# Performer attention and two MoE layers on one core: second products of the last layer moved by a tile, gate logits on column tiles, float64 conversion paced differently

## The chip, the cores and the metric

The program runs on one core of a Trainium2 chip. Its engines are TensorE (PE; its weight loads are shown as PEld), VectorE (DVE), ScalarE (ACT), GpSimd (POOL) and SyncE (SP, which issues most DMAs). Each works through its own instructions in order and waits on semaphores for the others. The metric is the time of one execution in device microseconds; less is better.

## The reference

```python
def phi(x):                       # q and k, scaled by 1/sqrt(sqrt(64)); omega is 128 x 64
    h = einsum('bhsd,md->bhsm', x, omega) - sum(x * x, -1, keepdims=True) / 2
    return exp(h - max(h, -1)) / sqrt(128)
kv  = einsum('bhsm,bhsd->bhmd', phi(k), v);  z = sum(phi(k), axis=2)
x   = (phi(q) @ kv) / (phi(q) @ z + 1e-6)    # 4 x 8 heads x 576 x 64 -> 2304 x 512
P   = exp(x @ w_gate - max)                  # 2304 x 8, then eight times:
#     P /= row sums;  P /= column sums;  P *= 2304 / 8
x   = sum over e of P[:, e:e+1] * (relu(x @ w1[e]) @ w2[e])   # 512 -> 1024 -> 512, 8 experts
h   = x @ w_in                               # 512 -> 2048, weights given as float64
out = (h - tanh(h)) @ w_out                  # 2048 -> 512, float64 weights, output float32
```

## The kernel before

**Attention** comes first, for about 211 us, and leaves x in DRAM as `xd[0]`. It is not changed but for a few instructions at its start.

**The first layer (experts)** takes three blocks of 768 tokens. Every large product is done in a split form: an operand is taken as a high part (cast on ScalarE, `split`, L81) and a low part (difference on VectorE or GpSimd, L82), and three products of these replace one. A block runs over 32 "quads" (8 experts x 4); a quad is seven first products (`product`, tiles a, b, e, L719) with sums and differences between them (tiles t, L742 to L773), which give four tiles h, and then six second products (`l2`, tile l, L836), one per 128 tokens. These six are queued in `ready` and taken out by `second(n)` between the first products of the next quad. Each adds its result into `acc` on VectorE (L856), weighted by the gate's column. At a quarter of a block (quad 8) the next block's x may be loaded (`xgo`); quads 9 and 10 then split it, largely on VectorE (L207, L82, L223).

**The second layer** takes the same three blocks of tokens. It runs over groups of four "shrinks" (`shrink`, tile p, 12 matmuls, L793). After each, u = p squared (ScalarE, L818) and u*p (VectorE, L819) start a polynomial for small values and tanh for the rest: four activations on ScalarE (L803 to L806), four VectorE instructions (L809 to L812). The last step, the split of the result into high h (ScalarE, L815) and low h (GpSimd, L816), is held back until the next shrink has issued its own instructions (`held`). The tiles t of a shrink have two buffers. After a group of four, three second products (l2, 12 matmuls each, for 128 tokens) are appended to `ready`; their results are added into `acc` on VectorE (L850). There are 4 x 2 groups per block, 24 in all, 96 shrinks. What order they get is set here, in the loop over f = 0 to 3:

```python
second(len(ready) - (3, 3, 2, 1)[f])
```

**Background work** is written as generators which `tick()` advances by a step: `wprep` loads and splits weights, `xprep` loads and splits x, and `bg` holds one of two more. First comes `gate`, during quads 0 to 5 of the first block: it loads x again in 12 pieces of 128 x 2 x 384 (`gx`, two buffers, issued on ScalarE's queue), makes logits transposed (8 x 384, L609), copies them, transposes them (L614), and normalizes the table `pt` eight times (tile cs, L649). Then comes `convert`, which turns the float64 weights into float32 by bit operations: 64 jobs, each with a load of `r` (L671), five steps of two VectorE instructions (L683 to L698), and a store. A step is taken at

```python
if bg and not pace[2] and (pace[1] == 1 or pace[0] * 3 % 8 < 3):
```

and `pace[2]` (L926) forbids it in some quads. The transposes of the first layer's finished result (`x2`, L868) wait in `turned`; `turn()` takes out one.

Of the kernel before, what the change touches and what calls it, by code (L numbers as in the profile page):

```python
# [9 lines left out]
F32 = mybir.dt.float32  # L10
# [3 lines left out]
ALU = mybir.AluOpType  # L14
AX = mybir.AxisListType
# [4 lines left out]
def performer_moe_kernel(ctx, tc, q, k, v, omega, wg, w1, w2, win64, wout64, out):  # L20
# [43 lines left out]
    ident = con.tile([P, P], F32, name="ident")  # L64
    ones = con.tile([P, P], F32, name="ones")
    bsq = con.tile([P, 3], F32, name="bsq")
    wgr = con.tile([P, NC, E], F32, name="wgr")
    pt = con.tile([P, NTT, E], F32, name="pt")


# [185 lines left out]
    with ExitStack() as actx, tc.manual_schedule():  # L256
# [44 lines left out]
        nc.scalar.dma_start(om2[:, 1, :], omega)  # L301
        load(0, 1)
        make_identity(nc, ident)
        nc.gpsimd.memset(qn[1][64:, 1:], 0.0)
        nc.gpsimd.memset(kn[1][64:, 1:], 0.0)
        load(1, 0, 1)
# [6 lines left out]
            nc.vector.memset(t[:, :, 1], 1.0)  # L313
        load(0, 2)
        load(1, 2)
        nc.sync.dma_start(wgr, wg.rearrange("(c p) e -> p c e", p=P))

        tps = bank("omT")
        nc.tensor.transpose(tps[:, :M], om2.rearrange("m a d -> m (a d)"), ident)
# [265 lines left out]
    def gate(gtp):  # L585
# [4 lines left out]

        def load(k):
            if k < 2 * NB:
                gx[k] = gtp.tile([P, 2, TB], F32, tag="gx", name=f"gx{k}", bufs=2)
                nc.scalar.dma_start(gx[k], src[:, k % 2, :, (k // 2) * TB : (k // 2 + 1) * TB])

        load(0)
        load(1)
        for _ in range(4):
            yield
        pl = lbank("lgT")  # L600
# [1 line left out]
        for k in range(2 * NB + 1):  # L602
            if k < 2 * NB:
                if k % 2 == 0:
                    ps = lbank(f"lg{k}")
                x = gx.pop(k)
                for c in range(2):
                    i = 2 * (k % 2) + c
                    nc.tensor.matmul(ps[:E, :TB], wgr[:, i], x[:, c], start=(i == 0), stop=(i == 3))  # L609
                load(k + 2)  # L610
            if lg is not None and k % 2 == 0:
                for i in range(TB // P):
                    t = (k // 2 - 1) * (TB // P) + i
                    nc.tensor.transpose(pl[:, E * t : E * (t + 1)], lg[:, i * P : (i + 1) * P], ident[:E, :E])  # L614
            if k % 2 and k < 2 * NB:
                lg = gtp.tile([E, TB], F32, tag="lg", name=f"lg{k}")
                nc.scalar.copy(lg, ps[:E, :TB])
            if k % 2:
                yield
        nc.vector.tensor_copy(pt, pl[:, : NTT * E].rearrange("p (t e) -> p t e", t=NTT))  # L620
# [260 lines left out]
    def tick():  # L881
        next(wprep, None)
        pace[0] += 1
        if pace[3] or pace[0] % 3 == 0:
            next(xprep, None)
        if bg and not pace[2] and (pace[1] == 1 or pace[0] * 3 % 8 < 3):
            try:
                next(bg[0])
            except StopIteration:
                bg.pop(0)  # L890
# [10 lines left out]
    def turn():  # L901
        if turned:
            turned.pop(0)()
# [11 lines left out]
    for st in stages:  # L915
        kind, s = st
        if kind == 0:
            for Q in range(NQ):
                e = Q // NQE
                if s == 0 and Q == NQE + 1:  # L920
# [2 lines left out]
                    phase.close()  # L923
                    pace[1] = 3
                    bg.append(convert(phase.enter_context(tc.tile_pool(name="cvp", bufs=1))))
                pace[2] = pace[1] > 1 and (Q == 0 or Q >= NQ - 2 or s == 0 and Q < NQE + 3)  # L926
                pace[3] = Q < 2 or Q == NQ - 1
                for i in range(7):
                    need(state["n1"] + i, u1, "w")
# [20 lines left out]
        else:  # L950
            for g in range(NGM):
                for j in range(2):
                    hh = []
                    for f in range(GF):
                        for i in range(2):
                            need(state["n1"] + 2 * f + i, u1, "w")
                            need(state["x0"] + 2 * j + i, ux, "x")
                        hh.append(shrink(state["n1"] + 2 * f, j, f"{s}_{g}_{j}_{f}"))
                        if j:
                            spent1.update(state["n1"] + 2 * f + i for i in range(2))  # L960
                        tick()
                        turn()
                        tick()
                        turn()
                        second(len(ready) - (3, 3, 2, 1)[f])
                    for t in range(3):
                        tt = 3 * j + t
                        ready.append(
# [45 lines left out]
```

## Time and profile before

| | us |
|---|---|
| median of three runs | 2248.67 |
| lowest, highest | 2242.39, 2251.53 |
| the profiled execution | 2249.2 |
| its span in the trace | 2247.4 |
| PE busy in the span | 2162.3 (96%) |
| DVE busy | 1792.7 (80%) |
| POOL busy | 1383.4 (62%) |
| ACT busy | 1057.9 (47%) |

Busy is the time in which an engine works at an instruction. TensorE's clock has two levels, 1.2 and 2.4 GHz; the view of windows gives the granted clock as a share of the higher one, and a matmul at the lower level is as busy as at the higher. In a timeline, equal instructions one behind another are merged (x6), and the brackets give the engine's idle time before an instruction and what ended it.

### The profile page before, as it was taken

To read this page: it belongs to the slowest core of one execution; us is meant where nothing else is said; L and a number is where in the kernel's file an instruction comes from. 1 tells how busy PE (TensorE), PEld (TensorE's weight loads), DVE (VectorE), ACT (ScalarE), POOL (GpSimd) and SP (SyncE) were. 2 spreads that over 40 slices of the span, in tenths; PEclk is the share of its full clock that TensorE was granted. 3 is DMA by queue.
4 is the path that set the end of the run, shared out by engine and by line. 5 is a ranking of instruction groups with operands and counts; after the bars stand their busy time and mean duration, and the time that the engine had idled before them with its cause. 6 is when DMAs were issued, how large, how long until landed. Compare 5 with 4: busy or idle time off the path is not lost.

```text
span 2247.4 us, 33143 instructions
## 1 busy us (share of the span) xinstructions
PE 2162.3 (96%) x10782; PEld 1903.3 (85%) x10782; DVE 1792.7 (80%) x3457; ACT 1057.9 (47%) x2577; POOL 1383.4 (62%) x1631
## 2 busy tenths in 40 slices
PE   8998999999999999999999999999999999999998
PEld 6786688899999899799999899899999887878887
DVE  8886487989998798899989798985555677777776
ACT  6775333333333433333333433333333577777775
POOL 5554476676767676676676767676666455454542
PEclk9999999999999999999999999999999999999999
DMA  4442313332323232323232323322122131221210
GB/s 113 126 124 88 111 59 101 104 95 87 103 78 97 92 99 88 104 94 103 79 103 80 101 85 104 106 87 74 59 76 66 61 111 45 99 71 54 88 43 29
DMA packets 184381, 195.70 MB, mean 87 GB/s; under 512 B 53392, under 2 KB 142992, under 8 KB 184208
## 3 DMA queue, kind: packets, MB, share of 16 engines
q1 hardware_dynamic: 177200, 184.09, 26.0%
q10 hardware_dynamic: 7008, 9.51, 1.3%
q8 instruction: 85, 1.39, 0.3%
q14 instruction: 88, 0.72, 0.1%
HBM read 171.00 MB, written 22.54 MB: 86 GB/s over the span
## 4 chain that ended last, share of the span: by engine, by line
PE 65%; DVE 9%; ACT 8%; issue 4%; POOL 3%; DMA 2%; SPq 0%; ACTq 0%; DVEq 0%; POOLq 0%
PE l L836 33%; PE b L719 12%; PE a L719 8%; PE e L719 8%; PE p L793 2%; POOL h L816 2%; DVE t L819 2%; ACT t L804 1%; ACT th L803 1%; ACT t L806 1%; ACT t L805 1%; POOL u L82 1%; ACT h L815 1%; DMA gx<-xd 1%; DVE acc L856 1%
## 5 line engine op out<-in xcount | busy, mean ns | idle before, releaser
L836 PE MATMUL l<-v,h 128*128 128x512 f32 x4320 | 1072.7, 395 | 35.1 <-ACT h L815 18.6
L836 PEld LDWEIGHTS l<-v,h 128*128 128x128 f32 x4320 | 807.5, 189 | 209.2 <-ACT h L815 25.3
L82 POOL TENSOR_TENSOR v<-rs,v 128x512 fp32r<-128x512 f32 x216 | 287.6, 1335 | 334.7 <-PE l L836 174.8
L856 DVE SCALAR_TENSOR_TENSOR acc<-l,pt,acc 128x512 f32<-128x512 f32 x540 | 397.6, 744 | 120.3 <-PE l L836 118.6
L82 POOL TENSOR_TENSOR u<-s,u 128x256 fp32r<-128x256 f32 x384 | 297.0, 784 | 132.7 <-ACT u L81 107.8
L719 PE MATMUL b<-x,u 128*128 128x384 f32 x1728 | 354.2, 340 | 11.1 <-DVE t L746 6.6
L719 PEld LDWEIGHTS b<-x,u 128*128 128x128 f32 x1728 | 309.9, 189 | 29.7 <-DVE t L746 9.7
L81 ACT CAST u<-s 128x256 fp32r<-128x256 f32 x384 | 154.2, 405 | 264.6 <-POOL s L161 236.4
L816 POOL TENSOR_TENSOR h<-t,h 128x384 fp32r<-128x384 f32 x96 | 112.5, 1172 | 238.4 <-ACT h L815 235.1
L82 POOL TENSOR_TENSOR u<-rq,u 128x256 fp32r<-128x256 f32 x288 | 228.5, 793 | 26.2 <-ACT u L81 24.9
L719 PE MATMUL a<-x,u 128*128 128x384 f32 x1152 | 234.4, 338 | 0.6 <-ACT xo L517 0.6
L719 PE MATMUL e<-x,u 128*128 128x384 f32 x1152 | 232.8, 336 | 0.0
L793 PE MATMUL p<-x,u 128*128 128x384 f32 x1152 | 226.0, 350 | 0.0
L793 PEld LDWEIGHTS p<-x,u 128*128 128x128 f32 x1152 | 216.2, 199 | 5.4
L719 PEld LDWEIGHTS a<-x,u 128*128 128x128 f32 x1152 | 206.3, 188 | 9.0 <-ACT xo L517 1.0
L719 PEld LDWEIGHTS e<-x,u 128*128 128x128 f32 x1152 | 203.6, 189 | 1.3 <-issue 1.3
L730 ACT ACTIVATE h<-b 128x384 fp32r<-128x384 f32 x96 | 47.2, 491 | 257.8 <-DVE b L768 254.5
L81 ACT CAST v<-rs 128x512 fp32r<-128x512 f32 x240 | 147.5, 621 | 37.6 <-PE l L836 36.9
L730 ACT ACTIVATE h<-t 128x384 fp32r<-128x384 f32 x96 | 50.4, 525 | 243.8 <-DVE t L755 243.8
L81 ACT CAST u<-rq 128x256 fp32r<-128x256 f32 x288 | 117.4, 408 | 1.6 <-ACT xo L870 1.6
L803 ACT ACTIVATE th<-p 128x384 f32<-128x384 f32 x96 | 47.2, 491 | 114.5 <-DVE t L819 114.5
L809 DVE TENSOR_TENSOR th<-p,th 128x384 f32<-128x384 f32 x96 | 53.6, 558 | 53.5 <-ACT th L803 53.5
(138 smaller groups left out, 3088.1 us busy)
## 6 DMA issues: line engine op xcount, KB each, us to landing
rq<-in_moe_w_dram SPq DMA_DIRECT2D x96, 512.0 KB, 4.0
rs<-in_moe_w_dram SPq DMA_DIRECT2D x192, 256.0 KB, 2.8
rqi<-win SPq DMA_DIRECT2D x24, 512.0 KB, 5.1
rs<-wout SPq DMA_DIRECT2D x48, 256.0 KB, 2.8
xt<-xd SPq DMA_DIRECT2D x24, 384.0 KB, 5.9
r<-in_moe_w_in_dram SPq DMA_DIRECT2D x32, 256.0 KB, 3.3
r<-in_moe_w_out_dram SPq DMA_DIRECT2D x32, 256.0 KB, 3.3
xd<-xo SPq DMA_DIRECT2D x32, 144.0 KB, 1.8
```

The source lines that it names most:

```text
L81: nc.scalar.copy(dst[:, 0], src)
L82: eng.tensor_tensor(dst[:, 1], src, dst[:, 0].bitcast(F32), ALU.subtract)
L719: nc.tensor.matmul(ps[:, :TB], u[:, wi, c], x[:, xi, c], start=(start and m == 0), stop=(stop and m == 5), skip_group_check=True,)
L730: nc.scalar.activation(h[:, 0], src, AF.Relu)
L793: nc.tensor.matmul(ps, u1[f + i][:, wi, c], ux[state["x0"] + 2 * t + i][:, xi, c], start=(m == 0), stop=(m == 11))
L803: nc.scalar.activation(th, ps, AF.Tanh)
L804: nc.scalar.activation(gb, u, AF.Square, bias=bsq[:, 1:2])
L809: nc.vector.tensor_tensor(th, ps, th, ALU.subtract)
L816: nc.gpsimd.tensor_tensor(lo, s, hi.bitcast(F32), ALU.subtract)
L819: nc.vector.tensor_tensor(s, u, ps, ALU.mult)
L836: nc.tensor.matmul(ps, hh[f][:, hi, t : t + P], u2[n + f][:, wi], start=(i == 0), stop=(i == len(todo) - 1))
L856: V.scalar_tensor_tensor(a, ps, p[:, e : e + 1], a, ALU.mult, ALU.add)
```

## The change

It has three parts. In the second layer `second` leaves one more product in the queue at the third and the fourth shrink, and the second `turn()` of each shrink is gone. In the gate, the four products of a piece of 384 tokens no longer add up in 8 rows of one bank: each goes to 32 columns of its own of TensorE's array and 32 rows of its own of the result (weights padded with zeros to 32 columns), and instead of a transpose a product with `sel` (128 x 8, each column with a one at its place in each of the four groups) sums the four and transposes at once. The pieces of x take the five buffers of `xtp` instead of two of their own, four ahead. The conversion takes 11 steps in 32 ticks instead of 12, may start one quad earlier, and rests in quads 9 and 10 of each block.

```diff
-    wgr = con.tile([P, NC, E], F32, name="wgr")
+    wgr = con.tile([P, NC, P // NC], F32, name="wgr")
+    sel = con.tile([P, E], F32, name="sel")
...
+        nc.vector.tensor_reduce(sel, ident.rearrange("p (g e) -> p e g", g=NC)[:, :E], AX.X, ALU.add)
...
+        nc.vector.memset(wgr, 0.0)
+        nc.sync.dma_start(wgr[:, :, :E], wg.rearrange("(c p) e -> p c e", p=P))
...
-                gx[k] = gtp.tile([P, 2, TB], F32, tag="gx", name=f"gx{k}", bufs=2)
+                gx[k] = xtp.tile([P, 2, TB], F32, tag="x", name=f"gx{k}")
...
-        load(0)
-        load(1)
+        for k in range(4):
+            load(k)
...
-                    nc.tensor.matmul(ps[:E, :TB], wgr[:, i], x[:, c], start=(i == 0), stop=(i == 3))
-                load(k + 2)
+                    g = P // NC * i
+                    nc.tensor.matmul(
+                        ps[g : g + P // NC, :TB], wgr[:, i], x[:, c], start=True, stop=True, tile_position=(0, g)
+                    )
+                load(k + 4)
...
-                    nc.tensor.transpose(pl[:, E * t : E * (t + 1)], lg[:, i * P : (i + 1) * P], ident[:E, :E])
+                    nc.tensor.matmul(
+                        pl[:, E * t : E * (t + 1)], lg[:, i * P : (i + 1) * P], sel, start=True, stop=True
+                    )
...
-                lg = gtp.tile([E, TB], F32, tag="lg", name=f"lg{k}")
-                nc.scalar.copy(lg, ps[:E, :TB])
+                lg = gtp.tile([P, TB], F32, tag="lg", name=f"lg{k}")
+                nc.scalar.copy(lg, ps[:, :TB])
...
-        if bg and not pace[2] and (pace[1] == 1 or pace[0] * 3 % 8 < 3):
+        if bg and not pace[2] and (pace[1] == 1 or pace[0] * 11 % 32 < 11):
...
-                pace[2] = pace[1] > 1 and (Q == 0 or Q >= NQ - 2 or s == 0 and Q < NQE + 3)
+                pace[2] = pace[1] > 1 and (Q == 0 or Q >= NQ - 2 or s == 0 and Q < NQE + 2 or NQ // 4 < Q < NQ // 4 + 3)
...
                         tick()
                         turn()
                         tick()
-                        turn()
-                        second(len(ready) - (3, 3, 2, 1)[f])
+                        second(len(ready) - (3, 3, 3, 2)[f])
```

How the instructions move, at three places. In these rows lines and buffer numbers are those of the two programs, so that L819 of before is L827 of after.

The SP queue where the conversion's first two loads (r) stand; rq and rs are loads of the experts' first and second weights. Before, row by row:

```order
L104 DMA rq<-in_moe_w_dram 128x4x256
L109 DMA rs<-in_moe_w_dram 128x512 x2
L104 DMA rq<-in_moe_w_dram 128x4x256
L109 DMA rs<-in_moe_w_dram 128x512 x2
L104 DMA rq<-in_moe_w_dram 128x4x256
L671 DMA r_0_4463<-in_moe_w_in_dram 128x512
L671 DMA r_1_4465<-in_moe_w_in_dram 128x512
L109 DMA rs<-in_moe_w_dram 128x512
```

After:

```order
L105 DMA rq<-in_moe_w_dram 128x4x256
L110 DMA rs<-in_moe_w_dram 128x512 x2
L105 DMA rq<-in_moe_w_dram 128x4x256
L110 DMA rs<-in_moe_w_dram 128x512
L679 DMA r_0_4300<-in_moe_w_in_dram 128x512
L679 DMA r_1_4302<-in_moe_w_in_dram 128x512
L110 DMA rs<-in_moe_w_dram 128x512
L105 DMA rq<-in_moe_w_dram 128x4x256
L110 DMA rs<-in_moe_w_dram 128x512
```

Before, the two loads of r come after 11 loads of rq and 20 of rs from the program's start; after, they come behind 9 of rq and 17 of rs.

VectorE in the second layer, from the end of the fourth shrink of a group (predicated copy into t) to the second shrink of the next; acc is the addition of a second product, t<-t,p is u*p. Before:

```order
L812 COPY_PREDICATED t_0_2_1_3_20796<-t_0_2_1_3_20793,th_2_1_3_20792 128x384
L850 TENSOR_TENSOR acc_0_1_20043<-l_20815,acc_0_1_20043 128x512
L819 TENSOR_TENSOR t_0_3_0_0_20850<-t_0_3_0_0_20847,p_3_0_0_20832 128x384
L809 TENSOR_TENSOR th_3_0_0_20846<-p_3_0_0_20832,th_3_0_0_20846 128x384
L810 SCALAR_TENSOR_TENSOR t_0_3_0_0_20850<-t_0_3_0_0_20849,t_0_3_0_0_20850 128x384
L811 SCALAR_TENSOR_TENSOR t_0_3_0_0_20850<-t_0_3_0_0_20848,t_0_3_0_0_20850 128x384
L812 COPY_PREDICATED t_0_3_0_0_20850<-t_0_3_0_0_20847,th_3_0_0_20846 128x384
L850 TENSOR_TENSOR acc_0_2_20109<-l_20869,acc_0_2_20109 128x512
L819 TENSOR_TENSOR t_0_3_0_1_20904<-t_0_3_0_1_20901,p_3_0_1_20886 128x384
```

After:

```order
L820 COPY_PREDICATED t_0_2_1_3_20782<-t_0_2_1_3_20779,th_2_1_3_20778 128x384
L858 TENSOR_TENSOR acc_0_0_20021<-l_20801,acc_0_0_20021 128x512
L827 TENSOR_TENSOR t_0_3_0_0_20836<-t_0_3_0_0_20833,p_3_0_0_20818 128x384
L817 TENSOR_TENSOR th_3_0_0_20832<-p_3_0_0_20818,th_3_0_0_20832 128x384
L818 SCALAR_TENSOR_TENSOR t_0_3_0_0_20836<-t_0_3_0_0_20835,t_0_3_0_0_20836 128x384
L819 SCALAR_TENSOR_TENSOR t_0_3_0_0_20836<-t_0_3_0_0_20834,t_0_3_0_0_20836 128x384
L820 COPY_PREDICATED t_0_3_0_0_20836<-t_0_3_0_0_20833,th_3_0_0_20832 128x384
L858 TENSOR_TENSOR acc_0_1_20094<-l_20855,acc_0_1_20094 128x512
L858 TENSOR_TENSOR acc_0_2_20115<-l_20872,acc_0_2_20115 128x512
L827 TENSOR_TENSOR t_0_3_0_1_20907<-t_0_3_0_1_20904,p_3_0_1_20889 128x384
```

An addition follows the fourth shrink in both; after the first shrink there are two in place of one.

VectorE in the second layer, behind the third shrink of a group where it also splits a weight tile v. Before:

```order
L812 COPY_PREDICATED t_0_2_1_2_20738<-t_0_2_1_2_20735,th_2_1_2_20734 128x384
L82 TENSOR_TENSOR v_20753<-rs,v_20753 128x512
L850 TENSOR_TENSOR acc_0_0_19988<-l_20761,acc_0_0_19988 128x512
L819 TENSOR_TENSOR t_0_2_1_3_20796<-t_0_2_1_3_20793,p_2_1_3_20778 128x384
L809 TENSOR_TENSOR th_2_1_3_20792<-p_2_1_3_20778,th_2_1_3_20792 128x384
```

After:

```order
L820 COPY_PREDICATED t_0_2_1_2_20741<-t_0_2_1_2_20738,th_2_1_2_20737 128x384
L83 TENSOR_TENSOR v_20756<-rs,v_20756 128x512
L827 TENSOR_TENSOR t_0_2_1_3_20782<-t_0_2_1_3_20779,p_2_1_3_20764 128x384
L817 TENSOR_TENSOR th_2_1_3_20778<-p_2_1_3_20764,th_2_1_3_20778 128x384
L818 SCALAR_TENSOR_TENSOR t_0_2_1_3_20782<-t_0_2_1_3_20781,t_0_2_1_3_20782 128x384
```

The addition between the split of v and the next u*p is gone from this place. On TensorE the four shrinks p and the three second products l of a group stood in the order p l p p l p l; they now stand in the order p l l p p p l. In the gate the order of TensorE's instructions stays as it was. The transposes x2 at the start of the second layer come one behind each of eight shrinks, where they came two behind each of four. In the whole program the last step of the conversion moves from quad 78 to quad 89, counted over the three blocks.

## Rows read from the trace of the kernel before

**Rows 1.** view of windows: us of stretch, busy per engine (x instructions), clock, DMA, GB/s.

```profile
211.74:261.40 49.66, 44.20 (x192) 26.47 (x192) 15.04 (x32) 14.24 (x36) 19.95 (x26) 1.00 0.48 144
347.28:369.01 21.73, 18.39 (x80) 16.36 (x78) 12.21 (x25) 5.95 (x15) 10.61 (x14) 0.84 0.22 73
384.65:421.42 36.77, 32.14 (x158) 28.02 (x157) 33.20 (x52) 11.01 (x28) 23.58 (x26) 1.00 0.37 122
499.84:687.47 187.63, 187.63 (x937) 169.31 (x936) 171.62 (x297) 68.27 (x168) 130.50 (x156) 1.00 0.30 93
895.18:934.50 39.32, 34.44 (x157) 30.07 (x156) 33.70 (x52) 10.96 (x28) 23.88 (x26) 0.91 0.35 110
1408.34:1442.10 33.76, 32.32 (x158) 27.88 (x157) 29.86 (x49) 11.01 (x28) 22.34 (x26) 1.00 0.40 133
1505.00:1677.00 172.00, 172.00 (x860) 155.17 (x859) 99.87 (x166) 64.21 (x155) 113.88 (x143) 1.00 0.21 68
1843.00:2217.00 374.00, 349.36 (x1653) 308.30 (x1654) 287.43 (x480) 276.86 (x594) 181.30 (x174) 0.96 0.20 65
```

**Rows 2.** waits of PE: who waited for whom, us in total, times, longest.

```profile
PE l L836 <- ACT h L815: 18.6, 12, 2.7
```

**Rows 3.** timeline of the last layer: start, us, engine, line, op, [idle before].

```profile
1785.80 0.55 DVE L819 TENSOR_TENSOR t<-t,p 128x384 f32<-128x384 f32 x1 [2.45 <-ACT t L818]
...
1878.25 0.56 DVE L819 TENSOR_TENSOR t<-t,p 128x384 f32<-128x384 f32 x1 [0.30 <-POOL h L816]
...
1889.97 2.92 PE L836 MATMUL l<-v,h 128*128 128x512 f32 x12
...
1891.18 1.25 DVE L82 TENSOR_TENSOR v<-rs,v 128x512 fp32r<-128x512 f32 x1
...
1892.35 0.67 DVE L850 TENSOR_TENSOR acc<-l,acc 128x512 f32<-128x512 f32 x1
...
1901.08 0.68 DVE L850 TENSOR_TENSOR acc<-l,acc 128x512 f32<-128x512 f32 x1
...
1902.05 0.56 DVE L819 TENSOR_TENSOR t<-t,p 128x384 f32<-128x384 f32 x1 [0.29 <-POOL h L816]
...
1915.44 0.56 DVE L819 TENSOR_TENSOR t<-t,p 128x384 f32<-128x384 f32 x1 [0.29 <-POOL h L816]
...
2234.07 0.73 PE L836 MATMUL l<-v,h 128*128 128x512 f32 x2 [1.72 <-ACT h L815]
```

**Rows 4.** timeline of the SP queue, 320 to 352 us.

```profile
323.15 12.96 SPq L109 DMA_DIRECT2D rs<-in_moe_w_dram  x2
...
349.80 0.93 SPq L671 DMA_DIRECT2D r<-in_moe_w_in_dram  x2
```

**Rows 5.** timeline of DVE at the first conversion step.

```profile
354.48 0.82 DVE L683 TENSOR_SCALAR ct<-r 128x256 uint32<-128x256 uint32 x1 [6.04 <-issue]
```

**Rows 6.** page, part 6: DMA issues, xcount, KB each, us to landing.

```profile
r<-in_moe_w_in_dram SPq DMA_DIRECT2D x32, 256.0 KB, 3.3
```

**Rows 7.** timeline of quads 9, 10 of blocks 0 and 1.

```profile
401.30 1.66 PE L836 MATMUL l<-v,h 128*128 128x512 f32 x6 [2.22 <-DVE acc L856]
...
407.51 1.37 DVE L697 TENSOR_SCALAR ct<-ce 128x256 f32<-128x256 uint32 x1
...
410.93 1.31 PE L719 MATMUL b<-x,u 128*128 128x384 f32 x6 [2.06 <-DVE t L746]
...
904.36 0.83 ACT L81 CAST x<-xt 128x768 fp32r<-128x768 f32 x1 [6.55 <-DMA xt<-xd]
...
909.96 2.29 PE L719 MATMUL b<-x,u 128*128 128x384 f32 x6 [3.84 <-DVE t L754]
```

**Rows 8.** groups by line, PE: xcount, busy, mean ns, idle before.

```profile
L609 PE MATMUL lg<-gx,wgr 128*8 128x384 f32 x48 | 17.3, 486 | 5.0 <-DMA gx<-xd 4.9
...
L649 PE MATMUL cs<-cs,ones 128*128 128x8 f32 x16 | 2.7, 241 | 3.5 <-DVE cs L645 3.4
L614 PE MATMUL lgT<-ident,lg 8*128 8x8 f32 x18 | 2.1, 209 | 0.0
```

More of the change, by code (lines that the diff above doesn't have):

```diff
@@ L315, in performer_moe_kernel @@
         load(1, 2)
-        nc.sync.dma_start(wgr, wg.rearrange("(c p) e -> p c e", p=P))
+        nc.vector.memset(wgr, 0.0)
+        nc.sync.dma_start(wgr[:, :, :E], wg.rearrange("(c p) e -> p c e", p=P))
         tps = bank("omT")
```

## The prediction

> **What bounds the kernel now.** I read the view of windows first, cut at the first matmul of a quad's product a [rows 1]. From quad 16 to quad 28 TensorE is busy all of 187.63 us: twelve quads at 15.63 us each, so in clean stretches of the first layer TensorE is the bound, although VectorE is busy 171.62 us of it. Four stretches are longer. Quad 7 takes 21.73 us instead of 15.63. The quads 9 and 10 of the three blocks of tokens (quads 9+10, 41+42, 73+74 in the count over blocks) take 36.77, 39.32 and 33.76 us instead of 31.27. The gate's stretch (quads 0 and 1) takes 49.66 us. The last layer (1843 to 2217) has TensorE busy 349.36 of 374 us, and its mean granted clock is 0.96.
>
> Then the waits of TensorE [rows 2]: the largest is that of second products for h, 18.6 us on ScalarE's part alone. It looks like the prize of the first part of the change. The timeline says otherwise. In the last layer each shrink begins on VectorE with u*p. From 1878.25 to 1915.44 eight shrinks pass, 37.19 us, 4.65 us each [rows 3]. TensorE does not set this pace: in the window it idles 24.6 us and loses about 15 us more to the lower of its two clock levels (0.04 of 374), so its own work at the full level would be some 334 of 374 us, about 33 us per eight shrinks. VectorE's u*p waits for POOL's h (0.30 and 0.29 us idle before it, ended by POOL h), POOL's h waits for ScalarE's cast of h, that cast stands in ScalarE's order behind the four activations of the next shrink, and those wait for VectorE's u*p. That is a ring over three engines which TensorE only feeds. A wait of TensorE for h inside it is the ring's spare time seen from the other side.
>
> **First part: the last block's second products one tile later.** The number of products, casts and additions is the same. On TensorE the product that stood behind the third shrink of four now stands behind the first shrink of the next four, as the second of two. Hence h is wanted one shrink later and the 18.6 us may well vanish from that line, or shift to another; but the ring turns at its own pace, so they are worth almost nothing by themselves. What counts is where the ring's own engines get other work. Per eight shrinks:
> - Twice VectorE now has two additions in a row (second order fence). One takes 0.68 us, and the row of 1901.08 ends at 1901.76 with 0.29 us idle before u*p at 1902.05 [rows 3]. A second one starts about 0.6 us after the first and overfills that gap by about 0.3 us: +0.6 for the two.
> - Once the addition behind a split of v goes (third fence). There VectorE has no spare time: the split of 1.25 us, then the addition, 0.67, with nothing idle between [rows 3]. About -0.6.
> - A fourth cast of u falls into a slot that had three. +0.1.
>
> So +0.1 us per eight shrinks, +1 us over the layer's twelve such groups; bounds -5 (the additions all hide) and +12 (1 us per group, as much as that costliest slot is over the others). The Trainium skill (SBUF — State Buffer, SBUF: two separate sides) states that VectorE and GpSimd take a shared pair of ports as an exclusive lock, held for the whole instruction by whichever starts first. By that rule a fourth split on POOL can hold VectorE up once more in each group, and the sum would be nearer the upper bound; the split of v at 1.25 us beside POOL agrees with it.
>
> At the layer's start the transposes of the first layer's result come one per shrink instead of two. Now u*p of the third shrink comes after 2.45 us idle on ScalarE's square, which stands behind two copies [rows 3]; half as many copies there, but some in shrinks that had none: -2 (bounds -6 and +2). At the end TensorE waits 1.72 us for the last h [rows 3]; one product more stands ahead of it, but that h comes no sooner: -1 (bounds -1.7 and 0). Sum of the part: -2 us.
>
> **Second part: the conversion.** Each step is two VectorE instructions as before, 320 steps. Three things move.
> - It starts in quad 5 instead of 6, and its first loads move on the SP queue past three slab loads and two quad loads (first fence). Now VectorE sits 6.04 us on the first load, which the SP queue only issued at 349.80 because it stood behind slab loads that waited for buffers [rows 4, 5]. After the change the loads stand behind the slab load issued at 323.15, ahead of the one that held the queue until about 336, while VectorE wants them one clean quad before 347.28, near 331. Such a load lands 3.3 us after issue [rows 6], so the wait goes: 21.73 - 15.63 = -6.1 us, lower clock level included (0.84 in that window). Bounds 0 and -6.1.
> - It pauses in quads 9 and 10 of each block, where the next block's x is split. First block: TensorE idles 2.22 us on an addition and 2.06 us on VectorE's t; conversion steps, one of them 1.37 us, stand right ahead [rows 7]. The second goes, of the first 1 us stays: -4.5 of the 5.5 that the pair is too long. Second block: the 3.84 us are mostly the load of x itself, since ScalarE idles 6.55 us on that DMA and VectorE behind it [rows 7]; conversion steps and the lower clock level (0.91 in that window) come on top: -4.3 of 8.05. Third: -2.0 of 2.49. Sum -10.8; bounds -6.8 (only the steps that stand right before a stall) and -16.0 (all the excess).
> - About eleven of 64 jobs move to quads 78 to 88. There VectorE is busy 99.87 of 172 us; with them it comes to the 171.62 of 187.63 under which TensorE did not idle [rows 1]. Nothing; if that cover fails, up to +2.5, a pair of quads like the third.
>
> **Third part: the gate.** Before, 24 products of 8 columns of weights run one behind another: 48 instructions, 17.3 us. 18 transposes take 2.1 us, and waits for gx 4.9 us [rows 8]. Afterwards four products stand on four column tiles of the array. No row shows column tiles. If they do not overlap: 0; if each pair runs as one: -8.65, half of 17.3. I take the middle, -4.3. The 18 selector products contract over 128 rows in full fp32, two instructions each: by the row of cs (16 instructions, 2.7 us) 36 take 6.1 us, +4.0; at the present 2.1 us, 0; I take +2.6, nearer to cs, which has the same shape. Four loads are issued ahead instead of two, and the issue no longer holds ScalarE until the last products are done: -3.5 of the 4.9 (bounds 0 and -4.9); not all, because the 12 loads of 384 KB still have to come beside the weights. Entering and leaving the tiles at 22 borders: 0 to +3.7 (0.17 us each, one whole small instruction by the row of cs); I take +0.8, near 0, since the borders of today's products show nothing of the kind. Sum -4.4; bounds -13.5 and +8. The rest of the chain behind the gate and the stages after it shift with it, since TensorE takes them up in order. The reduction that makes sel and the clearing of wgr stand at the very start, where TensorE waits for its first load anyway: nothing. The Trainium skill (TensorEngine Tiling (Array Packing), Key Properties) states that tiles run independently and that a change of the tiling mode drains the engine. By the first statement the gate comes out near its lower bound, by the second near the upper; no run here shows either yet.
>
> **Sum.** -2.0 - 6.1 - 10.8 - 4.4 = -23.3 us against the profiled execution's 2249.2 us (span 2247.4): 2225.9. The median of the runs shown is 0.5 lower, so 2225 us.
>
> **Rivals.**
> - Last layer bound by TensorE after all (0.08): then the deferral frees the idle time and the lost clock of [rows 1], up to 40 us over the layer: about 2187. For it: the largest wait of the whole trace is exactly this one. Against: where u*p idles in that group POOL's h or ScalarE ends it, never a product.
> - Column tiles give nothing and pay their borders (0.18): gate +4 instead of -4.4: 2233.
> - The conversion's stalls mostly stay (0.12): the first load still comes late (0 instead of -6.1) and the pauses bring only -6.8: 2235. For it: the second block's stall is a DMA's.
> - Slower (0.05): VectorE's two additions in a row. The second waits for the second of two products of about 2.8 us; VectorE has everything else of the ring queued behind it. Today the product begun at 1889.97 is over at 1892.89, 8.2 us ahead of its addition at 1901.08 [rows 3]. A second one of 2.9 us leaves 5.3; it decides if the lead falls by more than that: then up to 2.5 us are added in each of 23 half groups, +57, about 2282. Against: TensorE has some 4 us to spare in every eight shrinks.
>
> **How the numbers follow.** The forecast has 0.57. Its own range is 2212 to 2236 (the terms' bounds rarely fall on one side together). 0.5% is about what a measurement can tell from no change, 11.2 us: faster is below 2237.4. The forecast gives 0.55 of its 0.57 to faster, the gate rival 0.10 of 0.18, the conversion rival 0.05 of 0.12, the first rival all. Faster 0.78, same 0.16, slower 0.06. The range 2208 to 2240 leaves out the first rival, the slower one and the ends.
>
> **What would show it.** Quad 7 at 15.6 us and no long idle of VectorE before the first conversion step; the pairs at about 32, 35 and 31.8 us; the gate's stretch near 45 us with selector products of about 4.7 us; in the last layer a pace of 4.65 us per shrink, give or take 0.1, while TensorE's wait for h moves behind the fourth shrink. A pace below 4.5 us would refute the ring as the bound; a stretch of the gate above 50 us would refute the tiles' gain; a wait of TensorE of 2 us or more in quads 9 and 10 of the first block would refute the pauses' gain.

## The result

The changed kernel takes 2221.4 us (median of four runs, 2219.1 to 2222.7) against 2245.5 (2242.3 to 2251.5) for the kernel before, on the same chip: ratio 0.9888, 95% interval 0.9862 to 0.9915, so 24 us faster, with 19.1 to 31.0 as the interval. The forecast was 2225, in a range of 2208 to 2240. The two profiled executions stand 27.2 us apart (2249.2 and 2222.0; spans 2247.4 and 2220.2); the one of before is 3.7 us above its kernel's median, so about 3 of these 27.2 us belong to the execution and not to the change.

The sum came out near the forecast. But its terms for the gate and the ends of the last layer were off, and the term for the pauses was nearly right in size for another reason than the one given, as the experiments show. First the trace of the changed kernel. The view of windows, cut at the first matmul of a quad's product a, answers [rows 1] row by row (same columns):

```profile
209.74:249.91 40.17, 38.19 (x210) 27.56 (x210) 15.00 (x32) 14.18 (x36) 19.95 (x25) 1.00 0.53 178
336.04:351.68 15.64, 15.64 (x80) 14.11 (x79) 13.98 (x25) 6.13 (x15) 12.06 (x15) 1.00 0.28 94
367.32:398.60 31.28, 31.28 (x158) 28.22 (x157) 23.82 (x38) 12.12 (x30) 22.69 (x26) 1.00 0.36 118
476.80:664.48 187.68, 187.68 (x938) 169.33 (x937) 166.56 (x288) 68.06 (x168) 131.33 (x156) 1.00 0.28 89
872.21:908.25 36.04, 32.94 (x158) 29.54 (x157) 23.00 (x38) 12.17 (x30) 22.55 (x26) 0.95 0.33 106
1381.84:1413.12 31.28, 31.28 (x158) 28.22 (x157) 19.71 (x35) 12.37 (x30) 21.22 (x26) 1.00 0.39 127
1476.00:1648.00 172.00, 172.00 (x860) 155.19 (x859) 150.75 (x262) 63.08 (x154) 119.82 (x144) 1.00 0.27 88
1814.00:2188.00 374.00, 351.71 (x1696) 311.16 (x1696) 287.75 (x481) 278.02 (x596) 184.17 (x174) 0.97 0.20 65
```

- The gate's stretch has shrunk from 49.66 to 40.17 us.
- Quad 7 is a clean quad (TensorE busy in all of it), 15.64 us (was 21.73).
- Quads 9 and 10 take 31.28 us (was 36.77), 41 and 42 take 36.04 (was 39.32), 73 and 74 take 31.28 (was 33.76). In the first and the third block TensorE is busy in all of it. In the second it still idles about 3 us.
- The clean stretch is as it was, 15.64 us per quad. In the late quads, where the moved conversion steps now are, VectorE is busy for 150.75 of 172 us (99.87 before), and TensorE stays busy for all 172.
- In the last layer TensorE is as idle as before: 351.71 of 374 us busy, 349.36 before.

That last row already says that the deferral moved little. The waits of TensorE (who waited for whom, us in total, times, longest), which answer [rows 2]:

```profile
PE l L844 <- ACT h L823: 18.1, 13, 6.9
PE l L844 <- ACT xo L878: 9.2, 2, 4.9
PE l L844 <- POOL h L824: 7.6, 13, 0.7
...
PE l L844 <- DVE acc L856: 3.5, 2, 2.4
```

The wait for ScalarE's h was 18.6 us and is 18.1. Between the layer's ends it fell from 13.6 to 10.2 us (350 us of each trace), and a wait of 3.5 us for an addition (acc) came instead. At the layer's end it has grown from [rows 3]'s 1.72 to 6.9 us, and at its start the second products wait 9.2 us for copies of the transposed x (xo), where it was 1.7. Counted by place, the waits did not go away but moved: before, 26.1 of the 29.4 us that second products of this layer waited came behind the third shrink of four; now all but the 9.2 us come behind the fourth, 29.2 us with the end's 6.9.

The timeline of the last layer, u*p on VectorE, ring and end, answers [rows 3]:

```profile
1764.41 5.49 PE L844 MATMUL l<-v,h 128*128 128x512 f32 x12 [4.26 <-ACT xo L878]
...
1850.18 0.55 DVE L827 TENSOR_TENSOR t<-t,p 128x384 f32<-128x384 f32 x1 [0.30 <-POOL h L824]
...
1887.30 0.55 DVE L827 TENSOR_TENSOR t<-t,p 128x384 f32<-128x384 f32 x1 [0.31 <-POOL h L824]
...
1891.91 0.55 DVE L827 TENSOR_TENSOR t<-t,p 128x384 f32<-128x384 f32 x1
...
1929.01 0.55 DVE L827 TENSOR_TENSOR t<-t,p 128x384 f32<-128x384 f32 x1
...
2206.24 10.33 PE L844 MATMUL l<-v,h 128*128 128x512 f32 x36 [6.94 <-ACT h L823]
```

From 1891.91 to 1929.01 eight shrinks pass: 37.10 us, 4.64 each, against 4.65 before. The place of TensorE's second products has changed, and u*p still waits for GpSimd's h where it did (1850.18, 1887.30). The row at 1764.41 is the start of the layer: a second product waits 4.26 us for the copy of a transpose. The last one is the end: the final 36 matmuls begin after 6.94 us of idling and take 10.33 us; the granted clock of the window 2196 to 2217 is 0.84.

The groups of TensorE by line, 205 to 262 us (count, busy us, mean ns, idle before), answer [rows 8]:

```profile
L613 PE MATMUL lg<-gx,wgr 128*32 128x384 f32 x48 | 9.2, 497 | 1.5 <-DMA gx<-xd 1.5
...
L620 PE MATMUL lgT<-sel,lg 128*128 128x8 f32 x36 | 4.9, 257 | 0.0
```

The gate's products take 9.2 us in place of 17.3, the selector products 4.9 where the transposes took 2.1, the waits for gx 1.5 in place of 5.0.

The SP queue and VectorE at the first conversion step answer [rows 4, 5]:

```profile
300.76 10.05 SPq L110 DMA_DIRECT2D rs<-in_moe_w_dram  x2
...
312.35 0.86 SPq L679 DMA_DIRECT2D r<-in_moe_w_in_dram  x2
...
321.89 0.75 DVE L864 SCALAR_TENSOR_TENSOR acc<-l,pt,acc 128x512 f32<-128x512 f32 x1 [0.47 <-PE a L727]
322.56 0.85 DVE L691 TENSOR_SCALAR ct<-r 128x256 uint32<-128x256 uint32 x1
```

The load is issued at 312.35, and the first step stands 10 us later with no idle time in front of it.

Where the 27.2 us went, read from the starts of quads and of the dense layer in the two traces: gate -9.45, quad 7 -6.09, quads 9 to 11 of the three blocks -5.71, -3.55 and -2.71 (each sum takes in the quad behind the pair, which had been some 0.25 us over a clean one), attention -2.0, dense layer +2.0, the rest +0.3. The attention's 2 us are not shown to come from the change: the first quad starts at 209.7 to 212.4 us in the seven traces with the gate's part, which adds a few instructions at the attention's start, and at 211.6 to 212.8 us in the six without it. Each of these differences is read from one trace on either side. The gate's stretch repeats well with one exception: it is 48.9 to 49.6 us in the five traces with the old gate, and 39.6 to 40.2 in six of the seven with the new one; in the seventh (e4) it is 43.8, at a granted clock of 0.92. Quad 7 varies more, from 19.9 to 21.7 us in the four traces with the conversion's old start and rate.

### The profile page after: what moved, and what is told of

Read it like the earlier page. It is cut to its first block, busy times and chain, and to the rows that moved or that the text cites. A ratio compares the mean times of both kernels' runs of the same rounds, so it can differ in the third digit from the quotient of the medians.

```text
span 2220.2 us, 33171 instructions
## 1 busy us (share of the span) xinstructions
PE 2143.8 (97%) x10800; PEld 1898.6 (86%) x10800; DVE 1789.6 (81%) x3459; ACT 1059.2 (48%) x2577; POOL 1387.6 (63%) x1631
## 4 chain that ended last, share of the span: by engine, by line
PE 66%; ACT 10%; DVE 9%; issue 3%; POOL 2%; DMA 1%; DVEq 0%; SPq 0%; ACTq 0%; POOLq 0%
PE l L844 34%; PE b L727 13%; PE e L727 9%; PE a L727 8%; DVE t L827 2%; ACT t L812 2%; ACT th L811 2%; ACT t L814 2%; POOL h L824 1%; ACT t L813 1%; ACT h L823 1%; DVE t L819 1%; ACT v L82 1%; DVE t L818 1%; DVE acc L858 1%
## 5 line engine op out<-in xcount | busy, mean ns | idle before, releaser
L844 PE MATMUL l<-v,h 128*128 128x512 f32 x4320 | 1067.4, 396 | 39.8 <-ACT h L823 18.1
L801 PE MATMUL p<-x,u 128*128 128x384 f32 x1152 | 216.8, 344 | 0.0
L801 PEld LDWEIGHTS p<-x,u 128*128 128x128 f32 x1152 | 208.9, 194 | 3.4
```

The source lines that it names most:

```text
L801: nc.tensor.matmul(ps, u1[f + i][:, wi, c], ux[state["x0"] + 2 * t + i][:, xi, c], start=(m == 0), stop=(m == 11))
L844: nc.tensor.matmul(ps, hh[f][:, hi, t : t + P], u2[n + f][:, wi], start=(i == 0), stop=(i == len(todo) - 1))
```

## The experiments

All times are medians of four to eleven runs beside the kernel before on the same chip, unless said otherwise. Ratios are to the kernel before, with their 95% interval.

**Each part by itself.** e1 is the changed kernel with the deferral undone:

```
-                        second(len(ready) - (3, 3, 3, 2)[f])
+                        turn()
+                        second(len(ready) - (3, 3, 2, 1)[f])
```

> The changed kernel with its first part undone: the second products of the dense layer stand where they stood before, and the transposes come two per shrink again; gate and conversion stay changed. Theory (a ring over ScalarE, VectorE and GpSimd sets the pace): eight shrinks take 37.1 to 37.2 us as in both kernels, and the time is 2219 to 2221 us against 2221.4, since the second layer, from its first product to the end, took 473.7 us before and 475.7 after. Rival (TensorE's wait for h was the cost): the layer gets longer by 10 us or more, 2232 or above. Rival (the deferral did harm that other parts hid): below 2217.

Measured: 2220.6 us, ratio 0.9889 (0.9873 to 0.9904), beside 0.9888 with the deferral. Eight shrinks take 37.2 us. From its first product to TensorE's last the layer takes 473.3 us here, 472.0 to 474.5 in the other seven traces that have the old order and all products (the kernel before among them), and 475.0 and 473.6 in the changed kernel and in e6 below, which have the deferral. So the deferral is worth nothing that can be measured, neither in the time nor in the layer's own length: the theory held.

e2 is the kernel before with the gate's part alone, e3 with the conversion's part alone (the diff's lines for each, nothing else).

> The kernel before with the gate's part alone. Theory (the gain of the gate stays to the end, since TensorE takes the work in order): quads 0 and 1 take 40.2 us in place of 49.6, and the time falls by 9 to 10, to about 2236 from 2245.5. Rival (the weights' slabs are then late, or the conversion's first load stalls for longer, so part is given back): 2239 to 2243, with quad 7 longer than 21.7 us.

> The kernel before with the conversion's part alone. Theory: quad 7 falls from 21.7 to 15.6 us, the quads 9 to 11, 41 to 43 and 73 to 75 fall by 5.7, 3.6 and 2.7: 18 us in all, 2227.5. Rival (some of that came from the gate's earlier end, which gives the slab loads more lead): quad 7 or the second block's pair stay longer, 2231 to 2236.

Measured: e2 2238.1 us, ratio 0.9968 (0.9955 to 0.9981), -7 us; e3 2228.7 us, 0.9930 (0.9914 to 0.9945), -16 us. Together 23 of the 24 us. In e2 the gate's stretch is 40.0 us, and the conversion's first load is still late (quad 7: 20.8 us, not the longer one of the rival). The quads 9 and 10 become 1.8 us longer than before, but 41 and 42 become 2.1 us shorter, so the trace does not show that any of the gain is given back. The time lies between theory and rival. In e3 quad 7 takes 15.6 us and the three pairs 31.3, 35.2 and 31.3: the conversion's gain does not need the gate's.

**What sets the pace of the dense layer.** e8 leaves out a third of the second products (the product of h's low part), so TensorE has less to do and everything else is as it was. It ran a single time; the pace is read from its trace:

```
-        todo = [(hi, wi, f) for f in range(len(hh)) for hi, wi in ((0, 0), (0, 1), (1, 0))]
+        todo = [(hi, wi, f) for f in range(len(hh)) for hi, wi in ((0, 0), (0, 1), (1, 0))[: 3 - kind]]
```

> The changed kernel without the third of the three products (low part of h by high part of the weights) in the second products of the dense layer: 12 matmuls of 36 are left out for each four shrinks, some 2.8 us of TensorE's work, 5.6 us per eight shrinks. Theory (the ring sets the pace, TensorE has that time to spare): eight shrinks still take 37.1 us, and the time stays within 5 us of 2221, with TensorE idle for longer. Rival (TensorE with its waits sets the pace): 31.5 to 34 us per eight shrinks and 2155 to 2190.

Measured: 2218.9 us. The timeline of u*p, eight shrinks apart, and the window 1820 to 2170 (columns as above):

```profile
1849.88 0.55 DVE L827 TENSOR_TENSOR t<-t,p 128x384 f32<-128x384 f32 x1 [0.28 <-POOL h L824]
...
1886.95 0.55 DVE L827 TENSOR_TENSOR t<-t,p 128x384 f32<-128x384 f32 x1 [0.29 <-POOL h L824]
```

```profile
1820.00:2170.00 350.00, 290.32 (x1345) 256.04 (x1344) 269.60 (x449) 261.24 (x562) 176.96 (x168) 0.91 0.21 69
```

37.07 us per eight shrinks, the same as with all products. In the same window of the changed kernel TensorE is busy 329.21 us; here 290.32. Nearly 39 us of its work are gone and the time is the same: TensorE does not set the pace, as the theory had it.

e4 loosens a link of the ring. In the trace of the changed kernel, tanh starts at the end of u*p each time, and ScalarE's other three activations and the cast of h stand behind tanh. VectorE in turn waits for tanh, since it takes tanh's result first. The waits of ScalarE from 1820 to 2170, those of VectorE from 1843 to 2190, and the timeline of one shrink:

```profile
ACT th L811 <- DVE t L827: 85.8, 74, 2.3
```

```profile
DVE th L817 <- ACT th L811: 41.9, 75, 0.6
```

```profile
1890.86 0.48 ACT L826 ACTIVATE t<-p 128x384 f32<-128x384 f32 x1
...
1891.91 0.55 DVE L827 TENSOR_TENSOR t<-t,p 128x384 f32<-128x384 f32 x1
...
1892.49 0.49 ACT L811 ACTIVATE th<-p 128x384 f32<-128x384 f32 x1 [1.15 <-DVE t L827]
1892.88 0.61 ACT L812 ACTIVATE t<-t,bsq 128x384 f32<-128x384 f32 x1
...
1893.39 0.60 ACT L813 ACTIVATE t<-t,bsq 128x384 f32<-128x384 f32 x1
```

The two squares gb and ga need only ScalarE's own square of p. So they go ahead of tanh, and VectorE takes tanh's result third in place of first (the same edit in both lists):

```
-            nc.scalar.activation(th, ps, AF.Tanh)
             nc.scalar.activation(gb, u, AF.Square, bias=bsq[:, 1:2])
             nc.scalar.activation(ga, u, AF.Square, scale=CS, bias=bsq[:, 0:1])
+            nc.scalar.activation(th, ps, AF.Tanh)
...
-            nc.vector.tensor_tensor(th, ps, th, ALU.subtract)
             nc.vector.scalar_tensor_tensor(s, gb, B1, s, ALU.add, ALU.mult)
             nc.vector.scalar_tensor_tensor(s, ga, A1, s, ALU.add, ALU.mult)
+            nc.vector.tensor_tensor(th, ps, th, ALU.subtract)
```

> The changed kernel with one edit in the shrink: ScalarE does the two squares gb and ga before tanh, and VectorE uses tanh's result third in place of first. In the trace tanh starts each time at the end of VectorE's u*p (88.4 us of waits in 347), and everything else of ScalarE stands behind it; the two squares need only ScalarE's own result. Theory (the ring sets the pace, and this is a link of it): the pace falls from 4.64 us per shrink to what TensorE needs, some 4.2 (33.5 per eight), and the time by 30 to 42 us, to 2180 to 2191. Rival (TensorE with its lower clock and its waits for h is the bound): the pace stays at 4.6, the time within 5 us of 2221. Rival (VectorE is next, since th comes later and the copy behind it too): 4.4 us per shrink, about 2200.

Measured: 2179.0 us, ratio 0.9707 (0.9690 to 0.9723): 66 us below the kernel before and some 41 below the changed one, by the order of two lists. The timeline of u*p in e4, eight shrinks apart, and its window 1790 to 2140:

```profile
1852.19 0.54 DVE L827 TENSOR_TENSOR t<-t,p 128x384 f32<-128x384 f32 x1
...
1886.16 0.54 DVE L827 TENSOR_TENSOR t<-t,p 128x384 f32<-128x384 f32 x1
```

```profile
1790.00:2140.00 350.00, 347.59 (x1744) 312.82 (x1743) 323.97 (x486) 284.70 (x607) 194.01 (x181) 1.00 0.21 70
```

Eight shrinks take 33.97 us, 4.25 each, and TensorE is busy 347.59 of 350 us at a granted clock of 1.00. Now TensorE is the bound. The waits of ScalarE in e4, from 1800 to 2150:

```profile
ACT th L813 <- DVE t L827: 61.8, 77, 1.7
```

Tanh still waits for u*p in nearly every shrink, but the two squares are done by then. VectorE's wait for tanh, 41.9 us before the edit, is gone. The two lists were changed together, and neither was run alone, so how they share the gain is not shown.

Why tanh waits for u*p at all is argued from the kernel's lines, no run took it apart: the two instructions share nothing but p, which both read from the same PSUM bank. The Trainium skill (PSUM — Partial Sum Buffer, PSUM bank collisions raise a hardware error) states that two engines may not touch the same partitions of one bank at the same time, reads included, and that the compiler's scheduler puts a dependency between them. The trace agrees with such a dependency: u*p ends at 1891.91 + 0.55 = 1892.46 and tanh starts at 1892.49, and 74 such waits come to 85.8 us.

With TensorE as the bound the deferral might have become worth something. e5 is e4 with the deferral undone, by the lines of e1:

> The kernel of e4 (tanh behind the two squares) with the deferral undone. In e4 eight shrinks take 33.9 us and TensorE is the bound of the second layer. Theory (the deferral is worth something only where TensorE sets the pace, since then a wait for h is no longer spare time of the ring): 35 us or more per eight shrinks and 2187 to 2205 against 2179. Rival (worth nothing in either order, because h now comes earlier by itself): 2176 to 2183.

Measured: 2177.8 us, ratio 0.9699 (0.9686 to 0.9713); eight shrinks take 33.9 us. The rival was right: the deferral is worth nothing in either order. e4 and e5 can't be told apart, and both beat the kernel before and the changed one.

**What the gate's gain is made of.** e7 is the kernel before with the loads alone changed: gx from the pool of x, four ahead.

```
-                gx[k] = gtp.tile([P, 2, TB], F32, tag="gx", name=f"gx{k}", bufs=2)
+                gx[k] = xtp.tile([P, 2, TB], F32, tag="x", name=f"gx{k}")
...
-        load(0)
-        load(1)
+        for k in range(4):
+            load(k)
...
-                load(k + 2)
+                load(k + 4)
```

> The kernel before with the gate's loads alone changed: gx from the pool of x, four ahead in place of two; products, transposes and accumulation as before. Theory (the loads gave 3.4 us of the gate's 9.5, the column tiles the rest): quads 0 and 1 take about 46 us, the time 2241 to 2243. Rival (the loads gave most of it, since the products ran behind them): 41 to 43 us and 2237 to 2239. Rival (the loads gave nothing): 49.6 us, 2245.

Measured: 2242.7 us, ratio 0.9983 (0.9973 to 0.9992), about -4. Its groups of TensorE by line:

```profile
L609 PE MATMUL lg<-gx,wgr 128*8 128x384 f32 x48 | 17.3, 487 | 0.3 <-DMA gx<-xd 0.3
...
L614 PE MATMUL lgT<-ident,lg 8*128 8x8 f32 x18 | 2.1, 209 | 0.0
```

The products take 17.3 us as before, the waits for gx have gone from 5.0 to 0.3, and quads 0 and 1 take 44.4 us, between the theory's 46 and the rival's 41 to 43. So in the two traces the loads are worth 5.2 of the 9.45 us and the column tiles with the selector products the other 4.2: 8.1 less for the products, 2.8 more for the selector products, and 1.2 more waiting for gx, which shorter products wait for again.

**What the conversion's gain is made of.** e6 is the changed kernel without the new pauses:

```
-                pace[2] = ... (Q == 0 or Q >= NQ - 2 or s == 0 and Q < NQE + 2 or NQ // 4 < Q < NQ // 4 + 3)
+                pace[2] = ... (Q == 0 or Q >= NQ - 2 or s == 0 and Q < NQE + 2)
```

> The changed kernel without the conversion's new pauses; its start in quad 5 and everything else stay. Theory (early start and pauses are separate gains): quad 7 stays at 15.6 us, the quads 9 to 11, 41 to 43 and 73 to 75 go back towards 52.6, 55.2 and 49.6, and the time to 2230 to 2234. Rival (the second and third block's stalls come from the load of x, so the pauses matter in the first block alone): 2225 to 2229.

Measured: 2226.1 us, ratio 0.9919 (0.9903 to 0.9934): the pauses are worth 5 us (4.7 by the medians, 7 by the ratios, 4.6 in the quads of the traces), not the 10.8 of the prediction. The quads 9 to 11 of the three blocks take 50.7, 51.4 and 48.0 us, with the pauses 46.9, 51.7 and 46.9, before 52.6, 55.2 and 49.6. That is the rival's outcome: of the 4.6 us in the traces, 3.8 stand in the first block. The rest of these quads' gain, 7.4 of 12.0 us, comes without any pause. Three more kernels, each the kernel before with a single edit, looked for it: the earlier start, the rate of 11 steps in 32 ticks, the pauses. By the traces the start moves from quad 7 (first step at 354.48, in the quad from 347.28) to quad 6 (322.56, one quad ahead of the one from 336.04); the prediction and the expectations count these as 6 and 5.

> The kernel before, with the conversion started in quad 5 in place of 6 and nothing else: three steps in eight calls as before, no new pauses. Of the conversion's gain the pauses gave only 4.7 us (e6), so some 7 to 8 us beside quad 7's 6.1 are open. Theory A (the earlier start moves each step to another place of its quad, and away from the split of x): the traces show quad 7 at 15.6 us and the second block's quads 41 to 43 at 51 to 52 us, and the time falls by 10 to 12, to 2234 to 2236. Rival B (the wider rate does that): quad 7 at 15.6 us, the rest as before, 2239 to 2240.

> The kernel before with the conversion's rate alone changed, 11 steps in 32 calls in place of 12. Theory A (the rate as such gives nothing): quad 7 stays at 21 to 22 us, the pairs within 1 us of before, 2244 to 2247. Rival B (fewer steps in the quads where x is split): quads 41 to 43 at 51 to 52 us, 2238 to 2241.

> The kernel before with the new pauses in quads 9 and 10 of each block alone; start and rate as before. Theory (pauses are enough for the pairs by themselves): quads 9 to 11 fall from 52.6 to 46.9 us, 41 to 43 from 55.2 to about 51, 73 to 75 from 49.6 to 46.9, quad 7 stays at 21.7, and the time falls by 10 to 12, to 2234 to 2236. Rival (start and rate give most of the pairs' gain, pauses only the 4.7 us that e6 showed): 2239 to 2242.

Measured: start alone 2244.8 us (ratio 0.9992, 0.9983 to 1.0001), rate alone 2236.0 (0.9961, 0.9945 to 0.9976), pauses alone 2235.8 (0.9954, 0.9941 to 0.9967). Quad 7 and the sums of quads 9 to 11, 41 to 43 and 73 to 75, in us from the traces:

| kernel | 7 | 9-11 | 41-43 | 73-75 |
|---|---|---|---|---|
| before | 21.7 | 52.6 | 55.2 | 49.6 |
| start alone (e9) | 16.6 | 51.9 | 54.6 | 48.0 |
| rate alone (e10) | 16.3 | 51.6 | 50.8 | 47.8 |
| pauses alone (e11) | 20.1 | 47.7 | 48.3 | 46.9 |
| all three (e3) | 15.6 | 46.9 | 50.8 | 46.9 |

In e9 neither the theory nor the rival came out: quad 7 stays above 15.6 us and the time hardly falls. Theory A of e10 fell, the theory of e11 held in the time. The rate, which the prediction had at nothing, gives some 9 us alone, and the pauses about 10. All three give 16, not the sum, 21; by the table, rate and pauses both shorten the quads 41 to 43 and 73 to 75, and start and rate both shorten quad 7. Pauses alone even leave quads 41 to 43 shorter than all three do.

The early start alone brings nearly nothing, because the load still comes late for its step. The SP queue and VectorE of e9:

```profile
323.40 12.95 SPq L109 DMA_DIRECT2D rs<-in_moe_w_dram  x2
...
336.92 1.64 SPq L671 DMA_DIRECT2D r<-in_moe_w_in_dram  x2
...
334.60 0.56 DVE L746 TENSOR_TENSOR t<-b,t 128x384 f32<-128x384 f32 x1 [0.85 <-ACT v L81]
341.81 0.29 DVE L683 TENSOR_SCALAR ct<-r 128x256 uint32<-128x256 uint32 x1 [6.66 <-DMA r<-in_moe_w_in_dram]
```

With three steps in eight ticks, one load of rs and one of rq more stand ahead of the conversion's load in the SP queue than in the changed kernel, and this load of rs is the one that holds the queue for 13 us. The load is issued at 336.92 and VectorE sits 6.66 us on it. The step now falls in quad 6, which takes 17.8 us, and quad 7 takes 16.6: 3.1 us over two clean quads, where quad 7 alone was 6.1 over. The row of 334.60 suggests why it is not 6: the addition t<-b that TensorE needs next is done when VectorE begins to wait. In e10 VectorE's order is the same, it waits 5.2 us, and the quads 7 and 8 are 1.0 us over; in the kernel before, that addition stood behind the step:

```profile
356.09 0.55 DVE L746 TENSOR_TENSOR t<-b,t 128x384 f32<-128x384 f32 x1
```

In these three traces what such a wait costs goes with the instruction that is queued behind it.

## Why the prediction came out right, and where its steps were wrong

- **The bound of the last layer** was read rightly. e8 shows that TensorE's work can fall by 39 us in 350 with the pace unchanged, e1 that the wait for h is spare time of the ring. The forecast of 4.65 us per shrink came out at 4.64. The rule on the shared pair of ports of VectorE and GpSimd (the Trainium skill, SBUF — State Buffer, SBUF: two separate sides) would have put the sum nearer to +12; the trace does not bear that out, with 37.1 us per eight shrinks after and 37.2 before.
- **The ends of that layer** were to give -3 and gave none of it. The first eight shrinks took 45.46 us (44.56 before), in e6 44.67: nothing or a little worse, in place of -2. There the second products stand behind copies of transposes (1764.41, 4.26 us), and half as many transposes per shrink did not remove such waits. The end, from the last u*p to TensorE's last product, takes 14.6 and 14.8 us in the two traces with the deferral and 11.3 to 13.0 in the eight without it: +1.6 or more in place of -1. The step saw that one product more stands ahead of the last h; but then TensorE has nothing left, idles 6.94 us and runs the last 36 matmuls in 10.33 us, partly at the lower clock.
- **First conversion load, -6.1**: measured -6.09 and by the step's mechanism (issued at 312.35, no idle time). But the step named the earlier start as the cause. By itself that gives about 2 us (e9); e6, with the new rate and without pauses, has quad 7 at 15.6 us, so the place in the SP queue needs the rate as well. The start is in quad 6 in place of 7, where the step says 5 and 6; its times (331 and 347.28) are those of the right quads.
- **Pauses, -10.8, with the rate at nothing**: the three pairs with the quad behind them came out at -12.0, but the step that failed is this division. The pauses are worth 5 us beside the other two edits (e6); the rate, priced as "moved jobs, nothing", gives about 9 alone (e10), in its trace mostly in quad 7 and the quads 41 to 43. The step looked at which conversion step stood ahead of each stall, and took every step outside the two quads to stay in its place. A rate moves them all.
- **Moved jobs, nothing**: right in the late quads, where TensorE is busy 172.00 of 172.00 us.
- **Gate, -4.4**: -9.45 in the traces, -7.2 by e2's ratio (4.3 to 10.1). The term mis-sized is the column tiles' overlap, put at the middle, -4.3; it measures 17.3 - 9.2 = -8.1, nearly the bound of -8.65. Selector products came to +2.8 (+2.6 forecast), the waits for gx to -3.4 (-3.5). The borders, +0.8, show nowhere: selector products follow with no idle time, and the distances between starts of matmuls at a border are the same in both kernels (0.27 us into the gate's products where nothing is waited for, 0.42 us out of them). That tiles run independently (the Trainium skill, TensorEngine Tiling (Array Packing), Key Properties) agrees with the 9.2 us; a cost of the draining that the same section states can't be seen here.
- **The sum** hides these: in the two traces the gate gained 5 us more than its term, the conversion 1 more, and the dense layer came out 4 worse, chance of the two traces included. By the times of e2 and e3 it is some 3 more for the gate and about 1 less for the conversion. That 2225 lies 4 us from 2221.4 says nothing for the terms.

Of the signs named in advance, all but one came as put: quad 7, the pairs (the second within 1 us), the selector products, the pace, and the wait for h, which moved behind the fourth shrink, the longest of it to the end of the layer. The gate's stretch was to be near 45 us and was 40.

Open: how e4's gain is shared between ScalarE's list and VectorE's; whether the rate of 11 in 32 gains by fewer steps per quad or by other places of the steps in a quad; why quads 41 to 43 are shorter with pauses alone than with all three edits.

## What to carry to other kernels

Where an engine waits for a ring of other engines, its wait is no prize: look in the ring for a wait that holds up work which doesn't need it, such as one between two readers of one PSUM bank, and put that work ahead, on both engines (some 41 us here, against none for the deferral aimed at the largest wait). What a background step on a busy engine costs went here with the instruction queued right behind it, and start, rate and pauses did not add up, so they are measured one by one and together. Where terms stand at the middle of their bounds, a sum that comes out right is no proof of the terms.

## What was not expected of the hardware

- Products on four column tiles of 32: two of them (four instructions, 384 columns) go by in 0.84 us, against 1.46 us one behind another, here in the timelines of the changed kernel and of the kernel before:

```profile
216.23 0.85 PE L613 MATMUL lg<-gx,wgr 128*32 128x384 f32 x8
...
219.82 0.84 PE L613 MATMUL lg<-gx,wgr 128*32 128x384 f32 x4
...
223.38 0.84 PE L613 MATMUL lg<-gx,wgr 128*32 128x384 f32 x4 [1.48 <-DMA gx<-xd]
224.15 0.84 PE L620 MATMUL lgT<-sel,lg 128*128 128x8 f32 x6
```

```profile
225.34 0.35 PE L614 MATMUL lgT<-ident,lg 8*128 8x8 f32 x3
225.62 1.46 PE L609 MATMUL lg<-gx,wgr 128*8 128x384 f32 x4
```

  Where four of these products stand together, on all four column tiles (216.23), their eight instructions go by in 0.85 us. That is one place of eleven; at the other ten the products come in twos, at 0.84 us a pair, and no run put four together there.

- With less work on TensorE its granted clock was lower: in e8 (one execution) it is 0.91 in the window 1820 to 2170, against 0.98 of the changed kernel and 1.00 in e4, where TensorE is busy 347.59 of 350 us. In a layer that another engine paces this costs nothing, as e8's pace shows.
